# A gated attention and MLP kernel: the MLP's result loads and the output stores move from SyncE's DMA queue to GpSimd's

## The chip, the cores and the metric

The kernel runs on one core of a Trainium2 chip. The core has TensorE (PE in the profile), VectorE (DVE), ScalarE (ACT), GpSimd (POOL) and SyncE (SP), which run their own instruction streams and wait for each other by semaphores, and 16 DMA engines that move data between memory and the core. SP and POOL issue transfers; the engine that issues one goes on at once, and whoever needs the data waits for the transfer's semaphore. The metric is the device time in microseconds (us), as the median of the runs.

## The reference

For one sequence of 2048 tokens with 512 features, a gate mixes a sliding-window attention with an MLP:

```python
g = _sigmoid((x * gate_w).sum(-1, keepdims=True))
a = _A_ref(x, A_wqkv, A_wo)          # 32 heads of 16, each query sees the 256 newest keys
b = _B_ref(x, B_w1, B_b1, B_w2, B_b2)  # 512 -> 1792, gelu, -> 512
return g * a + (1 - g) * b
```

## The kernel before

The tokens are cut into 4 tiles of 512 (`T`), each into 4 blocks of 128 rows (`NB`), so that there are 16 blocks of output rows, numbered `nb`. All arrays are 32-bit; every dense product is made of three matmuls of split operands (`mm3`, lines 107 to 110), which stand in the profile as lines 108, 109 and 110.

Two streams of work are interleaved on TensorE. One is the attention: 128 units (8 groups of heads by 16 key blocks); each has the scores for the row maximum (`sm`, line 519, from `qd` and `kd`), the scores for the exponential (`st`, line 564, from `qs` and `ks`), ACT's exponential (line 586), and, for each tile, the product with the values (`pv`, line 608). The maxima run 12 units (`LEAD`) ahead of the rest, so `qd` and `kd` fall free before the attention ends. The other is the dense work: the projections of the four tiles, then the MLP in 8 rounds (`TURNS`: each half of the 1792 hidden features by each tile), then the final stage.

The result of an MLP round goes to memory, to `YA` for the first half and to `YB` for the second (`y_end`, line 812; the store at 816). The last round, for tile 3, keeps its four blocks on the core. The `YB` of tiles 0, 1 and 2 are loaded back by `load_y` (line 841) into `qd` and `kd`, two blocks of 128x512 to a load; this is called six times near the attention's end (line 979).

The attention's numerators and denominators go to memory (`ND`, line 636) and are divided by `att_norm` (line 642): the denominators are loaded (`den`, 646), inverted (650), stored (`RD`, 653), numerators and inverses loaded (`num` and `rb`, 658), multiplied (662), stored (`OT`, 665), and `load_part` loads them again (`ot`, 703), ACT and VectorE split them (706 and 709).

`final(t)` (line 857) makes a tile's output. For each block, ACT scales the MLP's result by 1 - g (`scale_y`, line 854, into `ao`), TensorE multiplies `ot` by `wo` (tile `a`; four turns of three matmuls for a block), VectorE adds g times that to `ao` (line 879), and SP stores the block (line 883). In the last tile the first two blocks share their first three turns ahead of their last ones, and the very last block is made and stored in two halves.

The order of each engine's instructions is the order in which the program records them. A planner with a clock of its own (`tick`, `after`, `need`) delays a step to its due time in nanoseconds or until what it needs was recorded; the chip keeps the order alone, not the due times. Every DMA of this kernel is issued by SP, in that order: a DMA that waits holds up all behind it. The core's scratch for DMA descriptions is set to 256 bytes when the program is created (line 1033, `dynamic_dma_scratch_size=256`). The kernel before issues no DMA from GpSimd, whose own work is the mask on the exponentials (line 580) and the row maxima's way into `qs` (line 546, a cast).

Of the kernel before, what the change touches and what calls it, by code (L numbers as in the profile page):

```python
# [19 lines left out]
NT = S // T  # L20
NB = T // 128
# [11 lines left out]
def gated_mix(ctx: ExitStack, tc: tile.TileContext, x, wqkv, wo, w1, b1, w2, b2, gate_w, out):  # L33
    nc = tc.nc
    x = x[0]
    out = out[0]
# [3 lines left out]
    cs = ctx.enter_context(tc.tile_pool(name="cs", bufs=1))  # L40
# [5 lines left out]
    def f32(ap):  # L46
        return ap.bitcast(F32)
# [20 lines left out]
    YB = [dr.tile([T, D], F32, name=f"YB{t}") for t in range(NT)]  # L68
# [15 lines left out]
    for r in (0, 64):  # L84
        for e in (0, 1):
            v = cut[r:r + 64, e]
# [7 lines left out]
    for s in (0, 1):  # L94
        for k in (0, 1):
            v = own[64 * s:64 * s + 4].rearrange("r (p s) -> r s p", s=2)[:, s]
# [10 lines left out]
    def mm3(p, lh, ll, rh, rl, first, last):  # L107
        nc.tensor.matmul(p, lh, rh, start=first, stop=False)  # L108
        nc.tensor.matmul(p, lh, rl, start=False, stop=False)  # L109
        nc.tensor.matmul(p, ll, rh, start=False, stop=last)  # L110
# [4 lines left out]
    def after(ns, fn, *args):  # L115
        now[1] += 1
        heapq.heappush(todo, (now[0] + ns, now[1], fn, args))
# [12 lines left out]
    def need(*keys):  # L130
        for key in keys:
            while key not in done:
                step_todo()
# [4 lines left out]
    def half_pt(name):  # L138

        if not spare:  # L140
            v = sb.tile([128, 2, 2, 320], F32, tag="pt", bufs=PTS, name=name)
            v = v.rearrange("p h a b -> p h (a b)")
            spare.extend(v[:, h, 0:T] for h in (1, 0))
        return spare.pop()
# [539 lines left out]
    def load_o(t, cs=range(NC)):  # L684

        if ("o", t) not in xts:
            if t == 0:
                v = sb.tile([128, NC, 2, T], F32R, tag="xt", bufs=1, name=f"ot{t}")
                xts["o", t] = [v[:, c] for c in range(NC)]
            else:  # L690
                xts["o", t] = {}
        for n, c in enumerate(cs):
            load_part(t, c, LAND0 if t == 0 else LANDO, 700 * n)
# [147 lines left out]
    def load_y(t, i):  # L841

        need(*[("y", 1, t, b) for b in range(NB)])
        if t < 2:
            v = f32(qd[:, t, i]).rearrange("p (j f) -> p j f", j=2)
        else:
            v = f32(kd[:, i, :, 0:T])
        nc.sync.dma_start(v, YB[t].rearrange("(i j p) f -> i p j f", j=2, p=128)[i])
        for j in range(2):
            ybs[t * NB + 2 * i + j] = v[:, j]  # L850

    def scale_y(nb, a):
# [4 lines left out]
    def final(t):  # L857
        if t == 0:
            load_o(1)
        ot = xts["o", t]  # L860
        parts = {}

        def begin(b, k, n):

            if b == 2 and t < 2:
                load_o(t + 2, range(NC - t))
            if b == 1 and t == 2:
                load_o(NT - 1, range(NC - 1, NC))
            if k == 0:
                parts[b] = half_pt(f"ao{t * NB + b}")  # L870
                after(0, scale_y, t * NB + b, parts[b])
            parts[b, k] = ps.tile([128, D // n], F32, tag="d", bufs=2, name=f"a{t}_{b}_{k}")

        def end(b, k, cs):
            nb, a, p = t * NB + b, parts[b], parts[b, k]

            def ev():
                need(("yb", nb))
                nc.vector.scalar_tensor_tensor(a[:, cs], p, g[:, nb:nb + 1], a[:, cs],
                                               op0=ALU.mult, op1=ALU.add)  # L880

            def store():
                nc.sync.dma_start(out[nb * 128:(nb + 1) * 128, cs], a[:, cs])
            after(100, ev), after(100 + (HOLDO if nb < NT * NB - 2 else 800), store)

        turns = [(b, c) for b in range(NB) for c in range(NC)]
        if t == NT - 1:
            turns[:2 * NC] = [(b, c) for h in (range(NC - 1), [NC - 1]) for b in (0, 1) for c in h]
        for b, c in turns:
            n = LASTN if t * NB + b == NT * NB - 1 else 1  # L890
            for k in range(n):
                if n > 1:
                    if c:
                        continue
                    row = range(NC)
                else:
                    row = [c]
                cs = slice(k * D // n, (k + 1) * D // n)
                if c == 0:
                    begin(b, k, n)  # L900
                for e in row:
                    need(("w", ("wo", e)), ("ot", t, e))
                    w, ts = wt["wo", e], slice(b * 128, (b + 1) * 128)
                    mm3(parts[b, k], ot[e][:, 0, ts], ot[e][:, 1, ts], w[:, 0, cs], w[:, 1, cs], e == 0, e == NC - 1)
                    yield MM3 / n
                if row[-1] == NC - 1:
                    end(b, k, cs)
# [35 lines left out]
    for u in range(-LEAD, NU):  # L943
# [33 lines left out]
        if u - NU + NKB == YAT:  # L977
            for k in range(6):
                after(1500 + YGAP * k, load_y, *divmod(k, 2))
    for n, c in enumerate(run):  # L980
# [38 lines left out]
PVAT = 2  # L1019
HELD = 2  # L1020
YAT = 5
YGAP = 2500
STEP = 2330.0
_TC = dict()
_INS = ["A_x", "A_wqkv", "A_wo", "B_w1", "B_b1", "B_w2", "B_b2", "gate_w"]
# [18 lines left out]
```

## Time and profile before

| | us |
|---|---|
| three runs | 751.10, 757.67, 749.64 |
| median | 751.1 |
| profiled execution | 749.65 |
| its span, from the first to the last instruction | 747.9 |

The page lists the busy time of each engine, the span in 40 slices, the DMA queues, the chain of work that ended last, the costliest groups of instructions and the DMA issues. In a row of a timeline stand start, duration, engine, line, operation, the tile written and the tile read, and, in brackets, the idle time before it with what ended it. "SPq" is the queue of DMA issues on SP; its durations are those of issuing, not of the transfer. A row of waits gives who waited for whom, the total in us, how often, and the longest.

### The profile page before, as it was taken

The page shows a single profiled execution, that of the slowest core. Times are in us where ns is not written, and L with a number is a line of the kernel's source. Part 1 is how long each engine was busy: PE and PEld are TensorE (multiplying, and loading weights), DVE is VectorE, ACT ScalarE, POOL GpSimd, SP SyncE. Part 2 cuts the span into 40 slices and gives each one's busy share as a digit, 9 for nine tenths or more (in the row PEclk, how much of TensorE's full clock was granted, in tenths as well). Part 3 has the DMA queues.
Part 4 walks back from the last instruction along what each step waited for, and adds up shares of the span by engine and source line. Part 5 has one row for each costly group of instructions (what it writes and reads, how often), then busy time and mean ns, then how long its engine had stood idle before and what let it go on. Part 6 is the DMA issues. An engine that isn't in the chain of part 4 may idle for free.

```text
span 747.9 us, 17961 instructions
## 1 busy us (share of the span) xinstructions
PE 732.7 (98%) x6129; PEld 604.4 (81%) x6129; DVE 520.1 (70%) x1567; ACT 421.5 (56%) x972; POOL 372.3 (50%) x846
## 2 busy tenths in 40 slices
PE   8999999998999999999999999999999999999998
PEld 7888888876788888888887877888888888867786
DVE  4532325799768867986798689768867986784552
ACT  4434532358537845864695478438745863794550
POOL 4200000339756865876577568747765875630000
PEclk9999999999999999999999999999999999999999
DMA  9889798998895687899575979996799799468572
GB/s 326 319 272 404 261 391 273 291 293 182 270 259 134 162 243 205 175 222 271 146 179 149 242 211 234 249 237 152 178 256 235 194 224 270 136 181 226 191 252 111
DMA packets 179260, 172.12 MB, mean 230 GB/s; under 512 B 56673, under 2 KB 122977, under 8 KB 179169
## 3 DMA queue, kind: packets, MB, share of 16 engines
q1 hardware_dynamic: 179168, 170.97, 81.4%
q8 instruction: 49, 0.80, 0.5%
q14 instruction: 43, 0.34, 0.1%
HBM read 108.53 MB, written 62.39 MB: 229 GB/s over the span
## 4 chain that ended last, share of the span: by engine, by line
PE 85%; DVE 5%; ACT 3%; issue 3%; DMA 2%; SPq 1%; POOL 1%; DVEq 0%; ACTq 0%
PE sm L519 9%; PE st L564 8%; PE pv_sm L608 7%; PE y L108 7%; PE y L109 6%; PE y L110 6%; PE u L108 5%; PE u L109 5%; PE u L110 5%; PE qk L110 4%; PE qk L108 4%; PE qk L109 4%; PE a L108 2%; DVE jm L524 2%; PE v L108 2%
## 5 line engine op out<-in xcount | busy, mean ns | idle before, releaser
L524 DVE CUSTOM_DVE_ANT_0 jm<-sm,mask 128x320 bf16<-128x320 f32 (+4 forms) x512 | 238.1, 465 | 95.3 <-PE sm L519 61.1
L580 POOL TENSOR_SCALAR_AFFINE_SELECT pt<-pt 64x256 f32<-64x256 f32 (+1 forms) x538 | 227.7, 443 | 108.5 <-ACT pt L586 98.1
L586 ACT ACTIVATE pt<-st 128x320 f32<-128x320 f32 (+4 forms) x512 | 199.6, 424 | 139.1 <-PE st L564 136.0
L519 PE MATMUL sm<-kd,qd 96*128 96x320 f32 (+4 forms) x512 | 153.9, 312 | 6.3 <-DVE M L524 5.5
L564 PE MATMUL st<-qs,ks 128*128 128x320 f32 (+4 forms) x512 | 153.9, 309 | 1.9 <-ACT pt L586 1.9
L546 POOL CAST qs<-tt 4x256 fp32r<-4x256 f32 x256 | 124.6, 487 | 53.3 <-DVE tt L539 42.7
L519 PEld LDWEIGHTS sm<-kd,qd 96*128 96x128 f32 x512 | 96.3, 188 | 33.2 <-DVE M L524 13.7
L564 PEld LDWEIGHTS st<-qs,ks 128*128 128x128 f32 x512 | 97.1, 190 | 18.8 <-ACT pt L586 3.2
L108 PE MATMUL y<-w,h 128*128 128x512 f32 x224 | 88.5, 395 | 0.0
L109 PE MATMUL y<-w,h 128*128 128x512 f32 x224 | 87.9, 393 | 0.0
L110 PE MATMUL y<-w,h 128*128 128x512 f32 x224 | 87.9, 392 | 0.0
L108 PE MATMUL u<-mx,w 128*128 128x512 f32 x196 | 80.0, 408 | 0.0
L109 PE MATMUL u<-mx,w 128*128 128x512 f32 x196 | 77.4, 395 | 0.0
L110 PE MATMUL u<-mx,w 128*128 128x512 f32 x196 | 77.1, 393 | 0.0
L608 PE MATMUL pv_sm<-pt,vbuf 64*32 64x320 f32 (+4 forms) x1408 | 73.6, 346 | 0.2
L608 PE MATMUL pv_st<-pt,vbuf 64*32 64x320 f32 (+4 forms) x1408 | 73.3, 346 | 0.0
L608 PEld LDWEIGHTS pv_sm<-pt,vbuf 64*32 64x32 f32 x1408 | 50.2, 106 | 20.2 <-issue 2.4
L325 DVE TENSOR_TENSOR qke<-qk,qke 128x512 fp32r<-128x512 f32 x32 | 22.0, 688 | 46.9 <-ACT qke L322 33.2
L322 ACT ACTIVATE qke<-qk 128x512 fp32r<-128x512 f32 x32 | 19.1, 597 | 56.2 <-PE qk L110 32.5
L110 PEld LDWEIGHTS y<-w,h 128*128 128x128 f32 x224 | 42.0, 188 | 9.8
L338 POOL MEMSET vx<- 128x32 f32 x16 | 2.4, 156 | 89.0 <-DMA SQ<-qke 44.5
L608 PEld LDWEIGHTS pv_st<-pt,vbuf 64*32 64x32 f32 x1408 | 46.1, 106 | 0.0
(148 smaller groups left out, 1332.7 us busy)
## 6 DMA issues: line engine op xcount, KB each, us to landing
kd<-SK SPq DMA_DIRECT2D x32, 384.0 KB
qs<-SQ SPq DMA_DIRECT2D x64, 192.0 KB
mx<-XT SPq DMA_DIRECT2D x24, 512.0 KB
SQ<-qke SPq DMA_DIRECT2D x16, 512.0 KB
SK<-qke SPq DMA_DIRECT2D x16, 512.0 KB
ND<-nd SPq DMA_DIRECT2D x32, 256.0 KB
raw_w<-in_B_w_dram SPq DMA_DIRECT2D x28, 256.0 KB
ks<-SK SPq DMA_DIRECT2D x32, 192.0 KB
```

What stands on the lines that cost most here:

```text
L108: nc.tensor.matmul(p, lh, rh, start=first, stop=False)
L109: nc.tensor.matmul(p, lh, rl, start=False, stop=False)
L110: nc.tensor.matmul(p, ll, rh, start=False, stop=last)
L322: nc.scalar.activation(e[:, h], p, AF.Copy)
L325: nc.vector.tensor_sub(e[:, 1 - h], p, f32(e[:, h]))
L519: nc.tensor.matmul(p[:, :w], qd[0:96, n, pr, 128 * j:128 * (j + 1)], kd[0:96, n, pr, k1 - w:k1], start=True, stop=True)
L524: nc.vector.tensor_tensor_reduce(junk[:, :w], p[:, :w], mask[:, 320 - w:320], 1.0, -3e38, ALU.add, ALU.max, M[:, 2 * (b % RB) + hb, pr:pr ...
L546: nc.gpsimd.tensor_copy(dst, src.unsqueeze(1).broadcast_to([4, 2, RB, 32]))
L564: nc.tensor.matmul(p[:, :w], ks[:, slot(g_, kb // NB), pr, at:at + 128], qs[:, pr, k0:k0 + w], start=True, stop=True)
L580: nc.gpsimd.affine_select(out=v, in_=v, pattern=[[0, v.shape[1]], [1 - 2 * e, 64]], compare_op=ALU.is_ge, fill=0.0, base=-e, channel_multi ...
L586: nc.scalar.activation(pt[:, hf, pr, :w], p[:, :w], AF.Exp, scale=SCALE)
L608: nc.tensor.matmul(pv[r // 64][32 * i:32 * i + 32, q - c * T:e - c * T], vts[g_, b // NB][r:r + 64, v:v + 32], rhs(r), start=start, stop=s ...
```

## The change

`load_y` loads each block of 128x512 by itself instead of two at a time, and issues the loads from GpSimd instead of SP: twelve of 256 KB where there were six of 512 KB. The planned distance between two calls of `load_y`, `YGAP`, goes from 2500 to 4500 ns. Of the 17 output stores, the 14 of blocks 0 to 13 are issued from GpSimd; block 14 and the two halves of block 15 stay on SP.

```diff
@@ load_y
-        nc.sync.dma_start(v, YB[t].rearrange("(i j p) f -> i p j f", j=2, p=128)[i])
         for j in range(2):
+            nc.gpsimd.dma_start(v[:, j], YB[t].rearrange("(i j p) f -> i p j f", j=2, p=128)[i][:, j])
             ybs[t * NB + 2 * i + j] = v[:, j]
@@ final
             def store():
-                nc.sync.dma_start(out[nb * 128:(nb + 1) * 128, cs], a[:, cs])
+                queue = nc.gpsimd if nb < NT * NB - 2 else nc.sync
+                queue.dma_start(out[nb * 128:(nb + 1) * 128, cs], a[:, cs])
@@
-YGAP = 2500
+YGAP = 4500
```

On GpSimd, at the end of the program, this is the difference between the two orders. `YB` are the MLP's results of a tile, `qd` and `kd` the buffers that take them, `ao` the finished rows, two blocks to a buffer.

```order
 L580 AFFINE_SELECT pt_3_9838<-pt_3_9838 64x2x64 x8
 L546 CAST qs<-tt 4x2x4x32 x8
-L1040 UNCONDITIONAL_BRANCH
-L1040 ISA
+L849 DMA qd<-YB_135 128x512 x4
+L849 DMA qd<-YB_136 128x512 x4
+L849 DMA kd<-YB_137 128x512 x4
+L884 DMA out_dram<-ao_10494 128x512 x2
+L884 DMA out_dram<-ao_10599 128x512 x2
+L884 DMA out_dram<-ao_10639 128x512 x2
```

Behind GpSimd's last compute instruction, where its program ended, the twelve loads now stand in one row, and behind them the fourteen stores, of which six are shown.

On SP, where the results were loaded, this stood before, with the division of the last tile's first part (`den`, `RD`, `num`, `rb`) and the next keys (`ks`) around the loads:

```order
L646 DMA den_3_10046<-ND_3_102 128x1x32
L848 DMA qd<-YB_135 128x2x512 x2
L848 DMA qd<-YB_136 128x2x512
L653 DMA RD_3_118<-den_3_10046 128x32
L848 DMA qd<-YB_136 128x2x512
L658 DMA num_3_10159<-ND_3_102 128x1x512
L658 DMA rb_3_10161<-RD_3_118 128x1x512
L848 DMA kd<-YB_137 128x2x512
L480 DMA ks<-SK_86 48x8x128
```

In the changed program the loads are gone from here, and this stands at the same place on SP:

```order
L646 DMA den_3_10046<-ND_3_102 128x1x32
L653 DMA RD_3_118<-den_3_10046 128x32
L658 DMA num_3_10159<-ND_3_102 128x1x512
L658 DMA rb_3_10161<-RD_3_118 128x1x512
L480 DMA ks<-SK_86 48x8x128
```

The division's four transfers and the next keys follow each other directly. In the final stage the stores have left SP in the same way, all but the last three. TensorE, VectorE and ScalarE have the same instructions in the same order as before.

## The prediction

> **What bounds the kernel now.** I read the page first, then the stretch that the change touches by windows (the columns are busy time and instruction counts, the granted clock, the share of the 16 DMA engines that was busy, and GB/s), then the waits of TensorE in it.
>
> ```profile
> span 747.9 us, 17961 instructions
> PE 732.7 (98%) x6129; PEld 604.4 (81%) x6129; DVE 520.1 (70%) x1567; ACT 421.5 (56%) x972; POOL 372.3 (50%) x846
> core 0: us, PE busy (x) PEld busy (x) DVE busy (x) ACT busy (x) POOL busy (x), PEclk, DMA share, GB/s
> 663.00:703.00 40.00, 38.80 (x437) 30.00 (x436) 22.36 (x47) 24.18 (x60) 0.00 (x0) 1.00 0.74 217
> 703.00:730.00 27.00, 27.00 (x121) 22.35 (x120) 16.13 (x25) 14.56 (x25) 0.00 (x0) 1.00 0.74 243
> 730.00:747.90 17.90, 14.59 (x75) 12.05 (x73) 5.25 (x8) 1.86 (x3) 0.00 (x0) 1.00 0.28 106
> PE st L564 <- ACT pt L586: 1.2, 1, 1.2
> PE a L108 <- DVE ao L879: 0.2, 1, 0.2
> ```
>
> TensorE is busy for 98% of the span. From 663 to 703 us, where the MLP's results are loaded, it lacks 1.2 us of 40, and that is one wait for the exponentials on ACT; from 703 to 730 it lacks nothing; the two rows of waits are the answer for 655 to 748 us. GpSimd is idle after 663 and the DMA engines are three quarters busy until 730, little after. So there is next to nothing to win here: no transfer that the change moves holds TensorE up. What it can do is end later than TensorE does, because all that follows the last matmul is this tail:
>
> ```profile
> 744.79 0.48 DVE L879 SCALAR_TENSOR_TENSOR ao<-a,g,ao 128x256 f32<-128x256 f32 x1 [0.88 <-PE a L110]
> 742.77 2.87 SPq L883 DMA_DIRECT2D out_dram<-ao  x3
> SPq L1040 <- DMA out_dram<-ao: 1.2, 1, 1.2
> ```
>
> The third store of the merged row is issued when the last VectorE operation ends (745.27) and has left SP at 742.77 + 2.87 = 745.64; SP then waits 1.2 us for it. The last result is in memory at 746.85, 1.1 us ahead of the end of the span. A store that lands after 746.85 lengthens the kernel by the difference.
>
> **What the change moves.** The rows of the two queues stand above, with the change. On GpSimd all twelve loads stand in one row behind the last cast, and fourteen stores behind them. The wider `YGAP` therefore does nothing to GpSimd's order: no other work of it stands between, and only data and the queue itself can space them. SP loses 6 loads and 14 stores, and the division's transfers close up.
>
> **SP's side.** What SP waited for in 670 to 748 us, and the parts of the last tile's division, which is the one chain of transfers with little slack:
>
> ```profile
> SPq L883 <- DVE ao L879: 17.2, 11, 4.3
> SPq L646 <- DMA ND<-nd: 10.7, 3, 4.7
> 705.06 0.40 SPq L636 DMA_DIRECT2D ND<-nd  x1
> 710.23 0.59 SPq L646 DMA_DIRECT2D den<-ND  x1
> 716.27 0.58 SPq L658 DMA_DIRECT2D rb<-RD  x1
> 716.96 1.81 SPq L703 DMA_DIRECT2D ot<-OT  x4
> 722.82 2.51 ACT L706 ACTIVATE ot<-ot 128x512 fp32r<-128x512 f32 x4 [7.71 <-DMA ot<-OT]
> 734.03 0.68 DVE L709 TENSOR_TENSOR ot<-ot 128x512 fp32r<-128x512 f32 x1
> 737.17 0.39 PE L108 MATMUL a<-wo,ot 128*128 128x512 f32 x1
> 738.05 1.43 DVE L879 SCALAR_TENSOR_TENSOR ao<-a,g,ao 128x512 f32<-128x512 f32 x2 [3.34 <-PE a L110]
> ```
>
> SP stood 17.2 us behind stores whose rows VectorE had not finished. That goes. But it ended no wait of TensorE: the last piece of the attention (`ot` of the last tile) is split at 734.71, and the matmuls that want it, the three whose result VectorE takes at 738.05, start at 737.17. This slack of 2.5 us grows if the loads at 716.96 land sooner and shrinks if the stores of the other queue take their engines; the bytes are the same, and they now come one at a time rather than five in a burst. I cost it at nothing; what is late next would be TensorE's own row. The gain is at most the waits shown, 1.2 + 0.2 us, and the larger of them is for an exponential, no transfer: I take 0.
>
> **GpSimd's side.** What does one transfer of 256 KB cost this queue? No row of before shows one, so I bound it.
>
> ```profile
> 657.31 5.49 POOL L546 CAST qs<-tt 4x256 fp32r<-4x256 f32 x8 [0.64 <-DVE tt L539]
> DMA  0000000000007989720000000695075001900000
> L546 POOL CAST qs<-tt 4x256 fp32r<-4x256 f32 x256 | 124.6, 487 | 53.3 <-DVE tt L539 42.7
> L182 POOL TENSOR_TENSOR w<-raw_w,w 128x512 fp32r<-128x512 f32 x5 | 6.8, 1352 | 22.0 <-DMA SQ<-qke 9.4 <-ACT w L178 6.8 <-DMA qs<-SQ 5.6
> ```
>
> The digits are the DMA engines' load in 736 to 748 us, 0.3 us a slice. The two 256 KB stores after 738.05 fill slices 12 to 18, 1.8 to 2.1 us for both, so 0.9 to 1.0 us of data each at full load. The last one, of 128 KB, took from 745.27 to 746.85, 1.6 us; half a store more of data makes 2.0 us for 256 KB on a quiet machine, from SP. On a busy one the `ND` store at 705.06 let its reader go at 710.23 (5.2 us), and the four loads from 716.96 let ACT go at 722.82 (5.9 us), both behind others in SP's queue.
>
> GpSimd adds the writing of the transfer's description, in software. Nearest rows: SP's issue (0.4 us in the `ND` row) and GpSimd's dearest operation on 128x512 (1.35). I take 0.7, between them and nearer to a cast (0.49) than to 1.35. With two queues at work an engine's data takes up to twice as long, so I add 0.8 us where the DMA share is 0.74, none where it is 0.28. If the queue takes one transfer at a time, that makes
>
> - busy (663 to 730): 2.0 + 0.7 + 0.8 = 3.5 us;
> - quiet (after 730): 2.0 + 0.7 = 2.7 us.
>
> Whether it is one at a time no row shows; the kernel sets the scratch for such descriptions to 256 bytes (line 1033), and that is why I take it so. The Trainium skill ("DMA: Bandwidth & Descriptors") gives 16 bytes to a descriptor ("Terms") and nine of them per engine and direction to a transfer over 128 partitions ("The descriptor swizzle"); if the 256 bytes are one engine's ring, sixteen fit, and a second transfer has no room beside the first. Its price for one, fixed 2.0 us plus the bytes ("Anatomy of one DMA"), would be an estimate of 2.6 us here; by it the loads would end at 694, the last store at 739.5 + 2.6 = 742.1, and the time would not change.
>
> Loads: 12 x 3.5 = 42 us from the last cast's end, 662.8, to 704.8. Who needs them:
>
> ```profile
> 697.45 0.72 ACT L854 ACTIVATE ao<-qd,g 128x512 f32<-128x512 f32 x1
> 703.76 0.74 DVE L879 SCALAR_TENSOR_TENSOR ao<-a,g,ao 128x512 f32<-128x512 f32 x1
> 714.40 0.71 ACT L854 ACTIVATE ao<-kd,g 128x512 f32<-128x512 f32 x1
> 725.23 1.94 ACT L854 ACTIVATE ao<-kd,g 128x512 f32<-128x512 f32 x3
> ```
>
> The first is read at 697.45 and lands at 666.3; the ninth (first of `kd`) at 714.40 and lands at 694.3; the twelfth about 726.5 and lands at 704.8. They are covered until a load costs (714.40 - 662.8) / 9 = 5.7 us; past that ACT, then VectorE, then TensorE's two result banks wait. Stores: the first block of rows is ready at 704.5, the queue is free at 704.8. Seven at 3.5 reach 729.3, seven at 2.7 reach 748.2. The thirteenth and fourteenth blocks are ready at about 738.8 and 739.5, so the queue, not the data, sets that end. Against 746.85 it is 1.35 us later.
>
> Sum: 0 (SP) + 0 (loads) + 1.35 (stores), on the profiled execution's 749.65 us, 1.7 us over its span: 751.0. That execution lies 1.45 us under the median of the three runs, 751.1; for the median I say 752.4.
>
> **Rivals.**
> - *The queue overlaps.* If GpSimd may describe the next transfer while one is in flight, each costs it only 0.4 to 1.35 us, under the 2.7 us in which TensorE finishes a block of rows (twelve matmuls at 27.0 / 121 = 0.22 us). The last store on it lands near 739.5 + 1.35 + 2.0 = 742.9, before 746.85: no change, 749.65 in the profile, 751.1 in the median. For it: nothing in the trace forbids it. Against it: the small scratch.
> - *Slower: the queue falls behind.* The 26 transfers in a row end at 662.8 + 26 s. Against 746.85 this decides at s = 84.05 / 26 = 3.23 us; each tenth more is 2.6 us, and 7.5 us (1%) is passed at 3.52 on average. My own mean is (19 x 3.5 + 7 x 2.7) / 26 = 3.28, so little is missing. With 1.35 us for the description: 4.15 and 3.35; loads until 712.6, four stores until 729.2, ten more until 762.7: 15.9 us late, 767 in the median. Dearer still, with the 5.2 us of the busy `ND` store until 730: loads until 725.2, one store until 730.4, thirteen at 3.35 until 774.0, 778 in the median. For it: 0.74 of the engines busy in two thirds of the stretch, and no row that shows what software takes to issue one. Against: SP's burst of stores, part of that load, is gone.
> - *VectorE holds the descriptions up.* VectorE works 22.36 of 40 us in the loads' stretch. If a transfer's description had to wait for one of its operations each time, 26 x 0.74 us (an `ao` operation) would be 19.2 us, if the queue is one at a time: with my 1.35, 772 in the median. The Trainium skill ("SBUF — State Buffer", "SBUF: two separate sides") has such a rule, for VectorE operations in a two-port mode, and it speaks against the change. No row of before shows it, as GpSimd did nothing there.
> - *Faster.* Needs TensorE's time before 663, or its clock, to change; both are untouched (clock 1.00 in all rows). At best 1.4 us, 749.7 in the median.
>
> **How the numbers follow.** One at a time at about my prices, up to the 1%: 0.40. Overlapping: 0.16. Slower by the queue's price: 0.33, by VectorE's hold: 0.07. Faster by over 1%: 0.04, for what I don't see. One per cent is about what a measurement of this kernel can tell from no change. So faster 0.04, same 0.56, slower 0.40. The range goes from 748.5 (the best case, less a microsecond of spread) to 768 (description at 1.35 us, with the spread); the dear end of both slow cases, about 0.13, and the faster one stay outside.
>
> **What would show it.** GpSimd's first load at 662.8 and not later; its rows 2.7 to 3.5 us apart if one at a time, under 1.4 if not; the end of its last store beside SP's; `L883`'s waits gone from SP, `L706`'s 7.71 shorter; TensorE's row for 703 to 730 still full. It is wrong if TensorE waits in the final stage for an `ao`, or if the gaps between GpSimd's rows are over 4 us.

## The result, and the profile after

| | before | after |
|---|---|---|
| median, us (6 runs each, side by side) | 750.69 | 762.31 |
| lowest to highest, us | 749.64 to 757.67 | 759.89 to 764.01 |
| profiled execution, us | 749.65 | 761.78 |
| its span, us | 747.9 | 760.1 |

The changed kernel takes 1.0151 times as long, 95% interval 1.013 to 1.0173: some 11.6 us more. In the profiles the spans differ by 12.2 us.

The stretch of the change by windows, kernel after (columns as in the prediction's windows):

```profile
663.00:703.00 40.00, 38.80 (x437) 30.03 (x436) 22.28 (x48) 24.18 (x61) 5.07 (x10) 1.00 0.66 188
703.00:715.00 12.00, 12.00 (x55) 9.92 (x54) 6.06 (x9) 4.61 (x8) 1.08 (x2) 1.00 0.75 229
715.00:720.00 5.00, 1.66 (x8) 1.04 (x6) 2.73 (x6) 4.33 (x7) 0.55 (x1) 0.98 0.40 145
720.00:725.00 5.00, 4.92 (x15) 3.94 (x16) 1.59 (x4) 0.00 (x0) 1.09 (x2) 0.67 0.73 232
725.00:730.00 5.00, 5.00 (x24) 4.13 (x23) 3.00 (x6) 3.31 (x6) 0.52 (x1) 1.00 0.52 190
```

Two things are new. Until 715 us TensorE is as full as before, but from 715 to 720 it works 1.66 of 5 us, and in the next 5 us it makes 15 matmuls where a full slice of the final stage has 24, at a granted clock of 0.67. And GpSimd, idle here before the change, issues to the end.

The rows of GpSimd's queue, from its timeline, kernel after: the last cast, the loads (L849), the stores (L884). Start and duration of the issue; the idle time in front is in brackets.

```profile
657.04 5.49 POOL L546 CAST qs<-tt 4x256 fp32r<-4x256 f32 x8 [0.64 <-DVE tt L539]
662.48 0.70 POOL L849 DMA_DIRECT2D qd<-YB  x1
666.25 0.55 POOL L849 DMA_DIRECT2D qd<-YB  x1 [3.07 <-issue]
...
678.58 0.54 POOL L849 DMA_DIRECT2D qd<-YB  x1 [2.88 <-PE st L564]
681.81 0.55 POOL L849 DMA_DIRECT2D qd<-YB  x1 [2.70 <-PE st L564]
...
690.94 0.55 POOL L849 DMA_DIRECT2D qd<-YB  x1 [4.18 <-issue]
697.21 0.55 POOL L849 DMA_DIRECT2D kd<-YB  x1 [5.72 <-issue]
700.53 0.54 POOL L849 DMA_DIRECT2D kd<-YB  x1 [2.77 <-issue]
706.69 0.54 POOL L849 DMA_DIRECT2D kd<-YB  x1 [5.62 <-issue]
712.76 0.54 POOL L849 DMA_DIRECT2D kd<-YB  x1 [5.53 <-issue]
717.30 0.55 POOL L884 DMA_DIRECT2D out_dram<-ao  x1 [4.01 <-issue]
...
740.60 0.55 POOL L884 DMA_DIRECT2D out_dram<-ao  x1 [2.03 <-DVE ot L709]
743.16 0.54 POOL L884 DMA_DIRECT2D out_dram<-ao  x1 [2.01 <-issue]
745.72 0.55 POOL L884 DMA_DIRECT2D out_dram<-ao  x1 [2.02 <-issue]
...
756.73 0.55 POOL L884 DMA_DIRECT2D out_dram<-ao  x1 [2.01 <-issue]
```

The description itself takes 0.54 to 0.56 us (0.70 the first time) throughout, and never are two rows closer than 2.56 us. That is what a queue with one transfer at a time would show; the runs with other sizes, below, bear it out. The twelve loads take (717.30 - 662.48) / 12 = 4.57 us each, from 3.2 (678.58 to 681.81) to 6.3 (690.94 to 697.21). A store in the quiet end takes 2.56 us at the least. The releasers in some brackets (`PE st`, `DVE ot`) are what ended nearest; the program has no such dependence. The last store, issued at 756.73, has landed some 2.56 us later by the rows ahead of it, at 759.3, 12.4 us after the last landing of before (746.85). That is the difference of the spans, 12.2 us, to within 0.3.

Next TensorE's stop. SP's timeline, kernel after, with an `OT` store and the load that waits for it, the last division's store and load of the denominators, and the last output stores:

```profile
699.66 0.38 SPq L665 DMA_DIRECT2D OT<-num  x1
705.88 0.32 SPq L703 DMA_DIRECT2D ot<-OT  x1
707.63 0.40 SPq L636 DMA_DIRECT2D ND<-nd  x1
714.55 0.60 SPq L646 DMA_DIRECT2D den<-ND  x1
...
747.72 2.88 SPq L884 DMA_DIRECT2D out_dram<-ao  x3
```

The first two of these rows in the kernel before:

```profile
699.44 0.32 SPq L665 DMA_DIRECT2D OT<-num  x1
703.31 0.32 SPq L703 DMA_DIRECT2D ot<-OT  x1
```

VectorE's timeline at the division, kernel after:

```profile
717.27 0.35 DVE L650 RECIPROCAL den<-den 128x32 f32<-128x32 f32 x1 [5.25 <-DMA den<-ND]
```

And TensorE's, from the last matmul ahead of the stop:

```profile
716.28 0.39 PE L110 MATMUL a<-wo,ot 128*128 128x512 f32 x1
720.08 0.80 PE L108 MATMUL a<-wo,ot 128*128 128x512 f32 x1 [3.41 <-DVE ao L879]
720.67 0.63 PE L109 MATMUL a<-wo,ot 128*128 128x512 f32 x1
```

SP's queue waits here for two stores in a row. The `OT` store holds its reader up for 6.2 us instead of 3.9 (705.88 - 699.66; 703.31 - 699.44), which is most of why the last division's `ND` store is issued 2.6 us later than before (707.63 against 705.06). That store then holds its own reader up for 6.9 us instead of 5.2 (714.55 - 707.63; 710.23 - 705.06), so `den` is loaded 4.3 us later. VectorE stands 5.25 us at the reciprocal (0.69 us before), and behind it, in order, wait line 709's halves of `ot` and the `ao` of line 879 that would free TensorE's result bank. TensorE stops for 3.41 us and then spaces its matmuls 0.43 us instead of 0.23 for a while. SP's last three stores end at 750.60 instead of 745.64, 5.0 us late: the stop and the slow matmuls behind it make up nearly all of that. In this kernel it is hidden: GpSimd's row ends later still. So the change has two prices, and the larger one covers the other.

### The profile page after: what moved, and what is told of

It is laid out like the page before. It is cut to its first block, busy times and chain, and to the rows that moved or that the text cites. A ratio compares the mean times of both kernels' runs of the same rounds, so it can differ in the third digit from the quotient of the medians.

```text
span 760.1 us, 17978 instructions
## 1 busy us (share of the span) xinstructions
PE 735.4 (97%) x6129; PEld 605.8 (80%) x6129; DVE 520.2 (68%) x1567; ACT 422.0 (56%) x972; POOL 386.6 (51%) x872
## 4 chain that ended last, share of the span: by engine, by line
PE 81%; issue 5%; DMA 5%; DVE 3%; ACT 3%; POOL 2%; SPq 1%; POOLq 0%; DVEq 0%; ACTq 0%
PE sm L519 9%; PE st L564 8%; PE pv_sm L608 7%; PE y L108 6%; PE y L109 6%; PE y L110 6%; PE u L108 6%; PE u L109 5%; PE u L110 5%; PE qk L110 4%; PE qk L108 4%; PE qk L109 4%; PE v L108 2%; PE v L110 2%; PE v L109 2%
```

## The experiments

"256" and "512" are the bytes of scratch for GpSimd's descriptions. Letters in the quoted expectations stand for theories, each with what it would give, and a letter can mean another theory in another run; the main ones are Q, the queue's one transfer at a time is the price, and B, the late transfers of the last division are. Each ratio, with its 95% interval, is to runs of the kernel before on the same chip (medians 749.81 to 751.18); it can differ by up to 0.2% from the ratio of the two medians.

### Loads alone

All stores back on SP; the loads as in the changed kernel.

```diff
-                queue = nc.gpsimd if nb < NT * NB - 2 else nc.sync
+                queue = nc.sync
```

> The twelve loads stay on GpSimd's queue in halves, all 17 output stores go back to SP. Theory Q (GpSimd describes a transfer only when the one before has landed; the row of 26 sets the end, and TensorE's lateness hides under it): the loads still end near 717 us, TensorE still stops for 3 to 4 us near 716 and its work ends 5 us late, and with no store behind the loads that is now what shows: 755 to 757 us. Rival T (the loads do no harm by themselves, only the stores queued behind them do): 750 to 752. Rival S (SP's stores hold the division up again on top of the late loads): 758 or more.

Measured: 754.91 us, ratio 1.0057 (1.0038 to 1.0076). The waits of VectorE and TensorE from 655 us on, this kernel (total in us, times, longest):

```profile
DVE den L650 <- DMA den<-ND: 6.3, 2, 5.7
PE a L108 <- DVE ao L879: 4.0, 2, 3.9
```

With the queue's long row gone the stop stands in the open and costs some 4.4 us of median. The time is at the lower edge of what Q gave (755 to 757), and for the reason that it gave, the stop; T's 750 to 752, by which the loads do no harm, did not come.

### Stores alone

The kernel before, with its fourteen stores on GpSimd.

```diff
-                nc.sync.dma_start(out[nb * 128:(nb + 1) * 128, cs], a[:, cs])
+                queue = nc.gpsimd if nb < NT * NB - 2 else nc.sync
+                queue.dma_start(out[nb * 128:(nb + 1) * 128, cs], a[:, cs])
```

> The six loads of 512 KB are on SP as before, the fourteen stores on GpSimd. Theory Q: the queue is empty when the first store comes (704 us), a store takes 2.6 to 3.0 us against the 2.7 us in which a block of rows is made, and the last one lands by 746: 750 to 752 us, and TensorE doesn't stop. Rival T (the stores are what costs): 757 or more. Rival V (VectorE's work holds the descriptions up): the rows of the stores on GpSimd are longer than 0.55 us and the time is over 753.

Measured: 753.27 us, ratio 1.0039 (1.0019 to 1.0059). GpSimd's first and last stores, from this kernel's timeline:

```profile
706.29 0.70 POOL L884 DMA_DIRECT2D out_dram<-ao  x1 [42.02 <-DVE ao L879]
712.14 0.55 POOL L884 DMA_DIRECT2D out_dram<-ao  x1 [5.15 <-DVE ot L709]
...
749.49 0.54 POOL L884 DMA_DIRECT2D out_dram<-ao  x1 [2.09 <-issue]
```

SP's last ones, same kernel:

```profile
744.83 2.88 SPq L884 DMA_DIRECT2D out_dram<-ao  x3
```

TensorE doesn't stop (its one wait in the final stage is 0.2 us, as before). Without loads ahead of it the queue is free at the first block, falls behind (5.85 us for the first store) and still ends after SP (749.49 + 2.6 against 747.71). Q holds in kind, but its 750 to 752 was too low, because its price for a busy store was. The longer rows of V did not come.

### Two transfers in flight, by 320 bytes

The whole change, with a scratch of 320 bytes; `z` takes `g1`'s memory to make room.

```diff
-    z = cs.tile([128, S // 128], F32, name="z")
+    z = g1
-    nc = ..., dynamic_dma_scratch_size=256)
+    nc = ..., dynamic_dma_scratch_size=320)
```

> The changed kernel with a scratch of 320 bytes in place of 256 (the sums of the gate share a buffer with the gate to make room). Theory Q with room for a second transfer beside the first: the loads come 2.2 to 3 us apart in place of 4.6 and end by 698, the stores keep up with TensorE, which doesn't stop: 750 to 752 us. Rival E (the DMA engines' share sets the pace, not the queue's depth): the loads stay 4 to 4.6 us apart and the time 758 to 762.

Measured: 758.36 us, ratio 1.009 (1.0056 to 1.0124). The second load is now described straight behind the first and the stores follow their data, so the depth does come from the scratch; but TensorE stops for 4.0 us, and the time is far above Q's. It is in E's range, but E's spacing of 4 us and more is not there: the twelve loads go out from 664.66 to 688.25, some 2 us apart. Neither side was right, and one reason was no part of either theory: see the run on the scratch alone, below.

### Halves of 64 partitions, 256 bytes

Each of GpSimd's transfers cut into two of 64 partitions, 52 of 128 KB.

```diff
+            for r in (0, 64):
+                nc.gpsimd.dma_start(v[r:r + 64, j], YB[t].rearrange(...)[i][r:r + 64, j])
...
+                    for r in (0, 64):
+                        queue.dma_start(out[nb * 128 + r:nb * 128 + r + 64, cs], a[r:r + 64, cs])
```

> The changed kernel with 256 bytes, each load and each GpSimd store cut into two of 64 partitions (52 transfers of 128 KB). Theory Q, by room for descriptors: three such pieces fit at once, so they overlap: loads end by 700, 750 to 754 us. Rival P (the queue takes one transfer at a time whatever its size, about 2 us fixed): 52 x 2.2 us and more from 662 makes 777 or more.

Measured: 757.43 us, ratio 1.0084 (1.0055 to 1.0113). GpSimd's first row of loads in this kernel's timeline:

```profile
664.24 1.71 POOL L850 DMA_DIRECT2D qd<-YB  x3
```

TensorE's wait in the final stage, same kernel:

```profile
PE a L108 <- DVE ao L880: 4.5, 2, 4.3
```

Three pieces, 384 KB, go out in one burst, within the same 256 bytes that hold one whole transfer of 256 KB. So what fits is set by the size of the description, not by a rule of one transfer. Fifty-two transfers end earlier than twenty-six (the last is issued at 749.73, against 756.73), which refutes P, a fixed price for each that adds up along the row. Q's 750 to 754 did not come either: the stop stays, although the last load is described at 700.96 instead of 712.76.

### Pieces and gap, all on SP

```diff
-            nc.gpsimd.dma_start(v[:, j], YB[t]...[i][:, j])
+            nc.sync.dma_start(v[:, j], YB[t]...[i][:, j])
-                queue = nc.gpsimd if nb < NT * NB - 2 else nc.sync
+                queue = nc.sync
```

> Only the pieces and the gap: twelve loads of 256 KB with the gap of 4500 ns, but on SP's queue, and all stores on SP. Theory C (the loads on a queue of their own take the engines from the division's transfers, which SP's own order would have kept apart): no stop of TensorE, 750 to 752 us. Rival L (what hurts is that the loads come late, into the last tile's division): the loads are late here too, TensorE stops for 2 us or more after 710, 753 us or more.

Measured: 750.55 us, ratio 1.0011 (0.9995 to 1.0027); TensorE's wait for `ao` is 0.2 us. SP's timeline, this kernel, at the last division:

```profile
708.64 0.40 SPq L636 DMA_DIRECT2D ND<-nd  x1
713.71 0.59 SPq L646 DMA_DIRECT2D den<-ND  x1
```

`ND` holds its reader up for 5.1 us, as before (5.2). The loads of 256 KB and the wider gap cost nothing that can be measured; the other queue is what counts.

### Stores with 320 bytes

The kernel before, with the stores on GpSimd and 320 bytes.

> The run with the stores alone on GpSimd, with a scratch of 320 bytes (the gate's sums share a buffer, as before). Theory Q (its 2.8 us over before are the row of stores taken one at a time): the stores follow TensorE 2.7 us apart and the last lands before SP's, 750 to 751 us. Rival G (GpSimd's stores cost by something else, such as the engines they share or the end of the program): 752.5 or more, as with 256 bytes.

Measured: 755.0 us, ratio 1.0062 (1.0034 to 1.0091). In the profile the queue is no longer last (the two last stores go out at 744.33, SP's end at 750.75) and from the last cast on it takes 85.8 us, before 85.1. But the last cast itself ended at 667.22 instead of 662.80, where the program is unchanged, and the time is in G's range. That lateness was open; the run on the scratch alone, below, shows it too.

### The reciprocal later

Loads alone as above, with the last division's reciprocal due 10000 ns after its start instead of 4500, so that VectorE has other work recorded ahead of it.

```diff
+        due = DIVS[c == NC - 1]
+        if (t, c) == (NT - 1, NC - 1):
+            due = (10000, 11200, 11700) + due[3:]
```

> The run with the loads alone on GpSimd, with the last division's reciprocal moved in VectorE's order behind six later operations (two splits and the end of the third block of rows among them), and with it the three transfers that follow it on SP. Theory H (TensorE stops because VectorE stands at this reciprocal, waiting for denominators that land late, with the ends of finished blocks queued behind it): the stop of 4 us is gone or under 1.5 us, 750 to 752 us. Rival B (the pieces of the attention themselves land too late): TensorE stops as long as before at the splits, 754 to 756 us.

Measured: 757.11 us, ratio 1.0095 (1.0075 to 1.0115). The waits in this kernel's final stage:

```profile
DVE num L662 <- DMA rb<-RD: 7.2, 2, 5.9
PE a L108 <- DVE ao L882: 4.7, 2, 4.5
```

The wait at the reciprocal went, and the next transfer of the chain, `rb`, took its place; TensorE stops for 4.5 us, some 10 us later in the program. Neither H's time nor B's came. The run doesn't separate the two: the edit moves the `RD` store on SP as well, and in this profile it goes out at 721.02, 2.9 us after the reciprocal ended (718.14), where in the loads alone it followed at once (720.05, 720.08). So part of the chain's lateness here is the edit's own.

### Eight loads

The changed kernel without the four loads of tile 2's MLP results (the ones into `kd`); its blocks are mixed with tile 0's results instead.

```diff
+        if t == 2:
+            v = f32(qd[:, 0, i]).rearrange("p (j f) -> p j f", j=2)
         for j in range(2):
-            nc.gpsimd.dma_start(v[:, j], YB[t]...[i][:, j])
+            if t < 2:
+                nc.gpsimd.dma_start(v[:, j], YB[t]...[i][:, j])
```

> The changed kernel without the four loads of tile 2's results (its output blocks are mixed with tile 0's instead, so that part of the result is another one). Theory Q: the row is four transfers shorter, the stores begin with the first finished block near 704 us and 14 x 3.2 us end near 750: 752 to 755 us; if the division is late only through the loads that are left out, TensorE doesn't stop. Rival D (eight loads on the second queue are enough to make the division late): TensorE still stops for 3 us or more, 755 to 758.

Measured: 757.61 us, ratio 1.0085 (1.0058 to 1.0111). The last load, the first store and the last, GpSimd's timeline of this kernel:

```profile
691.96 0.55 POOL L852 DMA_DIRECT2D qd<-YB  x1 [3.50 <-issue]
705.82 0.56 POOL L887 DMA_DIRECT2D out_dram<-ao  x1 [13.31 <-DVE ao L882]
...
752.55 0.55 POOL L887 DMA_DIRECT2D out_dram<-ao  x1 [2.01 <-issue]
```

TensorE behind its stop, same kernel:

```profile
719.34 0.50 PE L108 MATMUL a<-wo,ot 128*128 128x512 f32 x1 [1.50 <-DVE ao L882]
719.68 0.39 PE L109 MATMUL a<-wo,ot 128*128 128x512 f32 x1
```

With no load issued behind 691.96, the stop shrinks from 3.4 to 1.5 us. The queue is idle for 13.3 us ahead of its first store and still ends last (752.55 + 2.6): fourteen stores one at a time are too slow by themselves, as in the run of stores alone. The time is in D's range, but by the queue's end and not by D's stop of 3 us.

### The scratch's size alone

The kernel before, nothing on GpSimd's queue; only `z = g1` and 320 bytes.

> The kernel before, with nothing on GpSimd's queue; alone the scratch is 320 bytes and z shares g1's memory, as in the runs with two transfers in flight. In both of those the hardware queue took 85 to 86% of the engines' time for the same bytes (before: 81.4%), and the profile was 2 to 4.4 us late before the last cast, where the program is unchanged. Theory A (the 64 bytes by which the scratch grows move the tiles, and DMA gets dearer in the whole kernel): 753 to 755 us, hardware queue at 85 to 87%. Theory N (it is GpSimd's transfers in the tail, or spread between executions): 749 to 751.5 us, 81 to 82%.

Measured: 753.85 us, ratio 1.0034 (1.0016 to 1.0051). SP's queue in the page of the kernel before (packets, MB, share of the 16 engines' span):

```profile
q1 hardware_dynamic: 179168, 170.97, 81.4%
```

And in the page of this one:

```profile
q1 hardware_dynamic: 179168, 170.97, 87.6%
```

The same packets and bytes take 6 points more of the engines, in a kernel that issues no transfer from GpSimd at all. Theory A holds in its time and its share: 320 bytes, with `z` in `g1`'s memory, cost 3 us over the whole kernel. Whether it is the size, the 64 bytes by which tiles move, or the shared memory, no run separates; that it isn't a larger size as such is likely, as the stores alone have 80.2% with 512 bytes, below, and 79.7% with 256. So both runs with 320 bytes are to be read against this one, by the ratios, since the chips differ. The stores' 1.0062 is 0.3% above 1.0034, inside the intervals, and the whole change's 1.009 is 0.6% above, some 4 us. The stop of 4.0 us in the whole change with 320 bytes can't be put down to GpSimd's loads alone: here, without any, TensorE already waits 0.8 us for an `ao` where before it waited 0.2.

### Stores, whole change and loads with 512 bytes

512 bytes without moving `z`; the room comes from a mask that is held in bfloat16.

```diff
-    cut = cs.tile([128, 2, 64], F32, name="cut")
+    cut = cs.tile([128, 2, 64], BF16, name="cut")
-    nc = ..., dynamic_dma_scratch_size=256)
+    nc = ..., dynamic_dma_scratch_size=512)
```

Stores alone:

> The kernel before with 14 stores on GpSimd and 512 bytes of scratch (the mask cut in bfloat16 gives the space, z keeps its own). Theory Q (the short scratch alone makes the stores late): stores follow their data, the span ends with TensorE and SP, the tail behind the last cast 85 to 86.5 us; with theory A the time is then that of before, 749.5 to 751.5 us, with the hardware queue at 81 to 82%. If A is wrong and stores on GpSimd cost by themselves: 753 to 755.5 as in the run with 320 bytes.

The whole change:

> The whole change with 512 bytes of scratch. Queue's row no longer last. Theory B (the loads on a second queue make the last division's transfers late): TensorE still stops 3 to 4.5 us in the final stage, slower clock behind it, span ends with SP's last stores, tail behind the last cast 90 to 92.5 us, 754.5 to 757 us. Theory Q alone: no stop, 750 to 752 us.

Loads alone:

> The twelve loads alone on GpSimd, with 512 bytes of scratch; all stores on SP. The loads are then in by about 682 and no longer in flight when the last division's transfers go (from 705). Theory B (loads on a second queue cost time whether or not they are spread): 753.5 to 755.5 us, as the whole change with 512 bytes (754.9), and a profile with a stop of TensorE over 2 us in the final stage. Theory S (only their being spread over 55 us costs, since they then meet the division): 750 to 752 us, den's wait on VectorE under 3 us, TensorE's stop at most 1 us; the excess of the whole change with 512 bytes would then belong to loads and stores together.

| on GpSimd | 256 bytes | 512 bytes |
|---|---|---|
| loads | 754.91, 1.0057 (1.0038 to 1.0076) | 751.58, 1.0012 (0.9993 to 1.0031) |
| stores | 753.27, 1.0039 (1.0019 to 1.0059) | 751.40, 1.0010 (0.9991 to 1.0029) |
| both | 762.31, 1.0151 (1.0130 to 1.0173) | 754.92, 1.0046 (1.0026 to 1.0066) |

GpSimd's rows in the whole change with 512 bytes, by its timeline:

```profile
663.61 1.77 POOL L849 DMA_DIRECT2D qd<-YB  x3
...
679.54 0.54 POOL L849 DMA_DIRECT2D kd<-YB  x1 [3.02 <-issue]
705.72 0.55 POOL L884 DMA_DIRECT2D out_dram<-ao  x1 [25.64 <-DVE ao L879]
...
741.25 1.22 POOL L884 DMA_DIRECT2D out_dram<-ao  x2 [4.15 <-DVE ao L879]
```

Three loads go out within 1.77 us, the last at 679.54 instead of 712.76, and every store follows its `ao`; SP's last stores, issued until 744.79 + 2.88 = 747.67, end last. By the medians the depth takes both prices away when either half of the change stands alone, and 7.4 us of 11.6 when both do. So for the loads the time is that of theory S: not the second queue as such costs it, but that one at a time spreads the loads over 55 us.

What is left of the whole change, 4.2 us by the medians (754.92 against 750.74), looks like more than its parts together (0.4 + 0.7), but the intervals of the three ratios leave room for a plain sum. Its profiled execution is one of its quicker ones, 751.99 us, with a stop of 0.94 us, so the profile doesn't show where the rest goes. The profile of the loads with 512 bytes shows the converse, 754.72 us against a median of 751.58, and by windows a stop:

```profile
715.00:720.00 5.00, 2.88 (x14) 2.06 (x12) 2.89 (x6) 4.23 (x7) 0.00 (x0) 1.00 0.68 248
720.00:725.00 5.00, 5.00 (x15) 3.98 (x16) 1.51 (x3) 0.00 (x0) 0.00 (x0) 0.66 0.69 189
```

TensorE's timeline behind it, same kernel:

```profile
719.92 0.74 PE L108 MATMUL a<-wo,ot 128*128 128x512 f32 x1 [2.12 <-DVE ao L879]
```

That execution has the time and the stop of B, not of S, with all loads issued by 679.14. SP's timeline shows where its lateness began, at an earlier `ND` store:

```profile
677.84 1.36 SPq L636 DMA_DIRECT2D ND<-nd  x1
685.66 0.60 SPq L646 DMA_DIRECT2D den<-ND  x1
```

This store held its reader up for 7.8 us, the same one before for 4.4 (677.08 to 681.49), and the last division's `den`, at 714.28, was still late. So loads in a burst can set the chain back too; that they must meet the last division is not shown. The last division has so little room that single executions differ in it. With 512 bytes, 3 of 12 runs took over 753 us with the stores, 8 of 12 with both (beside them 2 of 29 of before), and 4 of 12 with the loads (2 of 17). That the stop is what makes those runs long is likely but not shown; it stays open.

## Why the prediction was off, point by point

The measured 762.31 us lies in the range, near its upper end, but the account with the highest chance, one at a time at about my prices and up to 1% slower (0.40), did not come. The rival "the queue falls behind" (0.33) did. And the range reached so far through a description of 1.35 us, which took 0.54: that its end covers the result is luck, as the time went into another term, the contention.

- *One at a time, because of the small scratch*: right. 256 bytes hold one transfer over 128 partitions; 64-partition pieces overlap in them, 320 bytes let two whole transfers go out together, 512 three. The rival of an overlapping queue, 751.1, hung on the scratch's size: with 512 bytes each part of the change alone gives it, the whole change (754.92) doesn't.
- *Description 0.7 us, quiet price 2.7*: right within 0.2; 0.54 to 0.56, and 2.56. The estimate of 2.6 that the prediction works out from the Trainium skill ("DMA: Bandwidth & Descriptors", "Anatomy of one DMA") agrees with the quiet rows, 2.56; the loads' mean of 4.57 is 2.0 us over it. My reading of the slices was high in one point: the digits add up to 4.2 slices, about 1.3 us for the two stores, so 0.6 to 0.7 us of data each at full load and not 0.9 to 1.0.
- *Busy price 3.5 us*: this is the term that was mis-sized. It was 4.57. My 0.8 for the contention with SP's transfers should have been 2.0 (4.57 - 2.56). That the busy machine sets this and not the direction of the transfer, the stores alone show: 4.1 us each from 706.29 to 730.89, 2.7 after. Twelve loads at 1.07 more are 12.8 us; the queue started 0.3 earlier, and the stores took 42.0 us (717.30 to 759.3) against 43.4 forecast. 748.2 + 12.8 - 0.3 - 1.4 = 759.3, which is where the last store landed. So the queue fell behind, at 662.48 + 26 x 3.72; that was to begin at 3.23 a transfer.
- *The bounds were there*: the busy `ND` store of before, 5.2 us, and the four loads, 5.9, were quoted as rows, and I built the price from the quiet end up. 4.57 lies between 3.5 and those, nearer the upper row than my value.
- *Loads covered until 5.7 us each*: right. No wait of ACT for a `YB` load shows; the ninth was issued at 697.21 and wanted at 714.40.
- *SP's side at nothing*: this step failed, though the time of the changed kernel doesn't show it. I named the slack of 2.5 us and that the other queue could take the engines, and then argued that one transfer at a time is gentler than five in a burst. The traces show the opposite for SP's chain, which waits for `OT` and then for `ND` to land. With GpSimd's loads in flight both took longer, 6.2 us instead of 3.9 and 6.9 instead of 5.2. These 4.1 us are nearly all of the 4.3 by which `den` was loaded late. The slack that counted was about 1 us, at `den` (see the next point), not the 2.5 us that I named for the last `ot`; the rest became the stop of 3.4 us. The loads alone show 6.1 and 6.8 us, the same pieces on SP 5.0 and 5.1. In the profiles without a load behind 704 us `ND` took 5.1 to 6.3 us, and 6.8 in the one of the whole change with 320 bytes, so the loads are the strongest cause of this in these runs, not the only one.
- *What the stop follows*: in all 13 profiles with VectorE's order unchanged, TensorE's wait for `ao` goes with the moment at which SP loads the last division's `den`, counted from the end of the last cast. Up to 48.4 us it is 0.2 us (five profiles, before among them at 47.4); at 48.8 and 49.1 it is 0.9 and 0.8; at 50.0, 1.5; at 50.7, 2.1; from 51.8 to 52.8, 3.4 to 4.3 (four profiles, the changed kernel at 52.0). This holds whichever of the transfers ahead of it was the late one.
- *TensorE's row for 703 to 730 still full*: wrong, as above. It was among the things that I said would show the prediction wrong, as were gaps over 4 us in GpSimd's rows; both came.
- *SP's waits gone, without a gain*: right. *YGAP without effect*: right on SP, by the run with pieces and gap together; on GpSimd no run changes it alone.
- *VectorE holds descriptions up*: this did not happen. The descriptions take 0.54 to 0.56 us in the stretch where VectorE works 22.28 of 40 us and where it is idle.

In the time: 752.4 for the median, 762.31 measured. The last store landed 11.1 us later than forecast (759.3 against 748.2), by the loads' 12.8 less 1.7 of the start and the stores; the median missed by 9.9, as it lay only 0.5 us above the profiled execution where I had added 1.45.

## What to carry to other kernels

A queue that holds one transfer has a price per link. On a busy machine this price is better bounded from the rows of like transfers on that busy machine (5.2 us here, and 4.57 came) than built up from the quiet price (3.5): with 26 links in a row, 0.4 us of error in the mean is 11 us. Before work moves to such a queue, look at what its spread will overlap, above all a chain of transfers with a slack of a few microseconds, and see whether its ring can be made deeper. A change of scratch or tile sizes needs its own run without the change under study, since it can move the time by itself.

## What the runs showed of the hardware

- *The clock after a stop.* In the changed kernel, behind a stop of 3.41 us, matmuls took 0.63 us instead of 0.39 and the granted clock was 0.67 in 720 to 725 us; after 2.12 us (loads, 512 bytes) also 0.63, with 0.66. All six stops of 2.12 to 4.51 us in the final stages of these kernels have some seven such matmuls behind them, in two (4.04 and 4.33 us) only after three faster ones. After 0.77, 0.94 and 1.50 us there were none, and the clock stayed at 1.00. So a stop of over 2 us here cost some 1.5 us more than itself: 5.0 us late for 3.41 in the changed kernel. The Trainium skill ("TensorE: Matmul & The Clock Gate", "Part 1: The HAM clock gate") has the clock drop after an idle window of about 3.4 us; the stop of 3.41 agrees, the one of 2.12 does not, and the measurement decides.
- *The share of the DMA engines moved by 6 points (81.4 to 87.6%) with 64 bytes of scratch and one small tile placed in another's memory*, and the time by 0.34%, with the same packets and bytes.
- *What fits into the scratch*: in 256 bytes one transfer over 128 partitions, or three over 64; in 320 bytes two over 128 were described within 1.24 us, in 512 three within 1.77.
